# Decode attention with a gated MLP: output weights in two groups, and the first load in two parts

## The chip, the cores and the metric

The kernel runs on one core of one Trainium2 chip. The core has five engines that run beside each other: PE (matrix products), DVE (vector work), ACT (scalar functions and copies), POOL (small general work) and SP, which only issues transfers and waits. Sixteen DMA engines move data between the large memory outside (HBM) and the on-chip memory of 128 partitions (SBUF). A queue of transfers belongs to the engine that issues them; here SP's queue (q1 in the profile) carries nearly all bytes, ACT's (q10) a few small inputs.

The metric is device time in microseconds (us), as the median of several runs. Before the change it is 1311.9 us, with three runs between 1311.33 and 1311.93.

## The reference

One token for each of two sequences attends over a cache of 32768 keys; the result is projected, multiplied with a gate from a small MLP, and added to the input.

```python
xn = _layernorm(x)                                   # x: 2 x 1 x 512
q = (xn @ wq).reshape(B, Sq, 32, 128).transpose(...)  # 32 heads of 128
k = jnp.repeat(k_cache, 4, axis=1)                   # 8 key heads, 32768 x 128 each, twice
v = jnp.repeat(v_cache, 4, axis=1)
p = _softmax(einsum("bhqd,bhkd->bhqk", q, k) * 128 ** -0.5)
s = einsum("bhqk,bhkd->bhqd", p, v).reshape(B, Sq, 32 * 128) @ wo
h = xn @ w1 + b1
y = square(max(h, 0)) @ w2 + b2                      # 512 -> 1792 -> 512
return x + s * silu(y)
```

All is float32. The two caches are 537 MB of the 561 MB that are read.

## The kernel before

A *stage* is one sequence and one key head: 16 stages, `s` = 0 to 15. A stage has 16 MB of keys and 16 MB of values, which come in two transfers of 8 MB each (64 KB to a partition), numbered `m` = 0 to 31 for either. Keys go through a ring of three slots of 32 KB (`kslots`), values through one buffer of 64 KB (`vbuf`). For each quarter stage `n` (0 to 63), `scores` (L240) transposes the keys on DVE (L249) and multiplies on PE (L254); `softmax`, `probs` and `values` (L307) follow, with the product of probabilities and values at L315. After the last value product of a stage, L322 to L327 bring the four heads of that stage into `oT`. So far this runs for every stage.

The output projection needs `oT` spread in another layout. This is done for groups of `WG` = 8 heads: after every second key head (L328) one DVE product (L331, `om`), one PE product (L334) and one ACT copy (L335) fill `oW[:, i]` for one sequence. The small selection tables `selj` and `sele` (L175 to L178) are made once and have the group's shape. `oW` is used only at the end, by `project` (L394 to L398), which multiplies it with the output weights, group by group in the order 0, 1, 2, 3.

All large transfers are listed in order in `loads` (L137 to L142) and are issued by SP in that order; each has an event that it waits for, given by `give` when the last reader of its buffer has been written down. A transfer that waits holds all behind it. The first in the list is the query weights `wq` (`load_wq`, L87): 8 MB into all of `vbuf`, 64 KB to a partition, in one transfer. Then come the first key halves (L97), the MLP weights and the caches. Last are the value chunks 30 (into two key slots) and 31 (into `vbuf`), and the output weights: four groups of 2 MB (16 KB to a partition), groups 0 and 1 in the third key slot as soon as the last keys are used, groups 2 and 3 in the first key slot after the first half of value chunk 30 has been multiplied. Group 3 comes in four pieces, of 8, 4, 2 and 2 KB to a partition (`PIECES`, L34), so that little work is left after the last one:

```python
for i in range(NWG - 1):
    project(i, 0, WG)
for j0, j1 in PIECES:
    project(NWG - 1, j0, j1)
```

Then two DVE products (L406, L407) and two stores (L409) end the program. The order on each engine and all waits are made by a scheduler from the program's order; it gives each transfer of SP and ACT one of eight completion counters in turn, so that a transfer also waits until the one eight places before it has landed.

Of the kernel before, what the change touches and what calls it, by code (L numbers as in the profile page):

```python
# [14 lines left out]
P = 128  # L15
# [15 lines left out]
NT = 4  # L31
HALF = 64 * 128
NEG = -3.0e38
PIECES = ((0, 4), (4, 6), (6, 7), (7, 8))  # L34


@with_exitstack
def gqa_decode_kernel(ctx: ExitStack, tc: tile.TileContext, x, kc, vc, wq, wo, w1, b1, w2, b2, out):
    nc = tc.nc
    B, _, D = x.shape  # L40
    _, HKV, SK, DH = kc.shape
    HQ = wq.shape[1] // DH
    REP = HQ // HKV
    F = w1.shape[1]
    ND = D // P
    NS = B * HKV
    NCH = SK // CHUNK
    FG = F // NG
    FJ = FG // 32
    DE = D // NG  # L50
    WG = 8
    NWG = HQ // WG
    SCALE = 1.0 / math.sqrt(DH)
    assert 4 * REP == 16 and D == 512 and DH == P and REP * DH == 512 and NCH == 2 and F == P * FJ and WG == 2 * REP

    x2 = x.rearrange("b s d -> (b s) d")
    out2 = out.rearrange("b s d -> (b s) d")
# [7 lines left out]
    def misc(name):  # L65
        return pms.tile([P, 512], F32, tag="ms", name=name)
# [19 lines left out]

    def load_wq(_):  # L87
        t = vbuf.rearrange("p (d f) -> p d f", d=ND)
        nc.sync.dma_start(vbuf, wq.rearrange("(p d) f -> p (d f)", p=P))
        return t  # L90

    def key_slot(n):
# [26 lines left out]


    def load_wo(i):
        if i % 2 == 0:
            wide[i // 2] = kslots[:, 2 - i].rearrange("p (i j e) -> p i j e", i=2, j=WG)
        t = wide[i // 2][:, i % 2]
        src = wo[i * WG * P:(i + 1) * WG * P, :].rearrange("(p j) e -> p j e", p=P)
        if i < NWG - 1:
            nc.sync.dma_start(t, src)
        else:
            for j0, j1 in PIECES:
                nc.sync.dma_start(t[:, j0:j1, :], src[:, j0:j1, :])  # L130
        return t

    wide = {}
    NK, NV = NS * NT, NS * NCH
    kslots = const.tile([P, 3, HALF], F32, name="kslots")
    vbuf = const.tile([P, 2 * HALF], F32, name="vbuf")
    loads = [(None, load_wq, 0), (None, load_half, 0), (None, load_half, 1), (("q", 0), load_w1, 0),  # L137
             (("s", 0), load_half, 2), (None, load_half, 3), (("q", 0), load_w2, 0)]
    for m in range(2, NV):
        loads += [(("s", 2 * m - 2), load_k, m), (("v", m - 3) if m > 2 else ("w", 1), load_v, m - 2)]  # L140
    loads += [(("s", NK - 2), load_v, NV - 2), (("v", NV - 3), load_v, NV - 1)]
    loads += [(("s", NK - 1), load_wo, 0), (("s", NK - 1), load_wo, 1), (("v", NV - 2), load_wo, 2), (("v", NV - 2), load_wo, 3)]  # L142
    past = {None}
    done = [0]

# [6 lines left out]
    def take(f, a):  # L152
        return tiles.pop((f, a))

    def give(*event):
        past.add(event)
        issue()
# [15 lines left out]
    for t in qz:  # L173
        nc.gpsimd.memset(t, 0.0)
    selj = const.tile([P, WG], F32, name="selj")  # L175
    nc.vector.tensor_reduce(selj, ident.rearrange("p (e j) -> p j e", j=WG), axis=AX.X, op=ALU.add)
    sele = const.tile([P, P // WG], F32, name="sele")
# [27 lines left out]


    wqt = take(load_wq, 0)
    for d in range(ND):
        for f in range(2):
# [6 lines left out]
    for f in range(2):  # L216
        for h in range(REP):
# [6 lines left out]
            v = t_ps.rearrange("p (e g y) -> p g e y", e=4, g=NG)  # L224
# [82 lines left out]
    def values(n):  # L307
        s, k = divmod(n, NCH)
        vt = take(load_v, n)
        o = o_ps[s % 2]  # L310
        for c in range(2):
            for i in range(NO // 4):
                for g in range(NG):
                    lo = (c * NG + g) * NO + 4 * i
                    nc.tensor.matmul(o[32 * g:32 * g + 16, :], pT[s][:, k, c, g, 4 * i:4 * i + 4, :].rearrange("p o h -> p (o h)"),  # L315
                                     vt[:, lo:lo + 4, :].rearrange("p o d -> p (o d)"),
                                     start=(k + c + i == 0), stop=(k == NCH - 1 and c == 1 and i == NO // 4 - 1))
        give("v", n)
        if k == NCH - 1:
            hkv, b = divmod(s, B)  # L320
            o_sb = work.tile([P, 512], F32, tag="o_sb", bufs=1, name=f"o_sb{s}")
            nc.scalar.copy(o_sb, o)  # L322
            t_ps = misc(f"oT_ps{s}")
            r4 = rs.pop(s)
            for i in range(4):
                nc.tensor.matmul(t_ps[:, :REP], o_sb[:, i * DH:(i + 1) * DH], r4[:, i, :], start=(i == 0), stop=(i == 3))  # L326
            nc.vector.tensor_copy(oT[:, hkv * REP:(hkv + 1) * REP, b], t_ps[:, :REP])  # L327
            if hkv % 2 == 1:  # L328
                i = hkv // 2
                m = work.tile([P, WG, P // WG], F32, tag="om", bufs=1, name=f"om{s}")  # L330
                nc.vector.tensor_mul(m, oT[:, i * WG:(i + 1) * WG, b:b + 1].to_broadcast([P, WG, P // WG]),  # L331
                                     sele[:, None, :].to_broadcast([P, WG, P // WG]))
                t_ps = misc(f"oW_ps{s}")
                nc.tensor.matmul(t_ps[:, :WG], m.rearrange("p h e -> p (h e)"), selj, start=True, stop=True)  # L334
                nc.scalar.copy(oW[:, i, :, b], t_ps[:, :WG])  # L335
# [36 lines left out]
    for n in range(NK):  # L372
        s, i = divmod(n, NT)
        if i == 0:
            set_q(s)
        scores(n)
        if n == 1:
            mlp_up()
        if n == 3:
            mlp_down()  # L380
        if i == 3:
            softmax(s)
        if n >= 5 and n % 2 == 1:
            values((n - 5) // 2)
        if i == 3:
            probs(s)
    values(NV - 2)
    values(NV - 1)


    a_ps = sc[0]
    wot = [take(load_wo, i) for i in range(NWG)]

    def project(i, j0, j1):  # L394
        for j in range(j0, j1):
            for g in range(NG):
                nc.tensor.matmul(a_ps[32 * g:32 * g + 32, :DE], oW[:, i, j, :], wot[i][:, j, g * DE:(g + 1) * DE],  # L397
                                 start=(i == 0 and j == 0), stop=(i == NWG - 1 and j == WG - 1))  # L398
# [5 lines that stand above are left out]
# [29 lines left out]
```

## Time and profile before

| what | us |
|---|---|
| median of three runs | 1311.9 |
| the profiled execution's own time | 1312.29 |
| its span, first to last instruction | 1310.2 |
| PE busy | 912.5 |
| DVE busy | 669.9 |
| ACT busy | 130.3 |
| first transfer issued (L89) | 0.73 |
| query weights landed, first product with them (L212) | 22.79 |
| output weights: first of seven transfers issued | 1257.76 |
| last product of the projection done, DVE starts L406 | 1306.52 |

The profiled execution lies 0.4 us over the median; 2.1 us of it lie outside the span. In the lists of the profile a line gives the time of an operation's start in the span, its duration, the engine, the line of the program, and output and inputs; "x8" counts instructions. PE counts each product of float32 twice. SPq and ACTq are the two queues that issue transfers. In the table of windows the last three numbers of a row are PE's granted clock, the mean busy share of the sixteen DMA engines (packets are counted where they begin, so that a short window can show over 1.00) and the rate in GB/s.

### The profile page before, as it was taken

How to read it: one execution, taken by the hardware profiler on the slowest of the kernel's cores; microseconds unless marked ns; L12 is line 12 of the kernel's file. 1: busy time of each engine (PE TensorE's matmuls, PEld its weight loads, DVE VectorE, ACT ScalarE, POOL GpSimd, SP SyncE). 2: the span in 40 equal slices, each digit the busy share in tenths (PEclk: the TensorE clock that was granted, in tenths of full speed). 3: DMA queues.
4: the chain of work that ended last, by engine and by line, in shares of the span. 5: the costliest groups of instructions: out<-in, count | busy, mean ns of one | idle time of the engine just before them, and what ended most of it. 6: DMA issues, size and time to landing. Idle time of an engine off the chain costs nothing.

```text
span 1310.2 us, 11827 instructions
## 1 busy us (share of the span) xinstructions
PE 912.5 (70%) x5054; PEld 230.9 (18%) x5054; DVE 669.9 (51%) x778; ACT 130.3 (10%) x429; POOL 14.9 (1%) x76
## 2 busy tenths in 40 slices
PE   3777675758857677775758767576885767777575
PEld 1221121212202121120212112121220212111023
DVE  2866654446655445665445565444665544566410
ACT  0020010201002020110202001020110202001020
POOL 0000000000000000000000000000000000000000
PEclk9988877888878898887889878778987879888888
DMA  9999999999999999999999999999999999999997
GB/s 404 432 441 435 429 439 426 435 430 433 433 432 433 437 431 433 429 437 429 435 435 427 439 424 439 428 437 437 427 437 428 433 435 431 435 429 431 427 435 307
DMA packets 11042, 561.76 MB, mean 429 GB/s; under 512 B 1239, under 2 KB 1259, under 8 KB 1646
## 3 DMA queue, kind: packets, MB, share of 16 engines
q1 hardware_dynamic: 10952, 561.00, 99.2%
q8 instruction: 39, 0.64, 0.2%
q14 instruction: 13, 0.11, 0.0%
q10 hardware_dynamic: 38, 0.02, 0.0%
HBM read 561.01 MB, written 0.00 MB: 428 GB/s over the span
## 4 chain that ended last, share of the span: by engine, by line
DMA 72%; DVE 21%; issue 4%; PE 3%; ACT 0%; SPq 0%; DVEq 0%
DMA kslots<-in_A_k_cache 66%; DVE kt L249 20%; DMA kslots<-in_A_wo 2%; DMA kslots<-in_A_v_cache 2%; DMA vbuf<-in_A_wq 2%; PE sc L212 1%; PE sc L254 1%; PE o_ps L315 0%; PE y_ps L364 0%; PE h_ps L346 0%; ACT p L275 0%; DVE qr L219 0%; ACT pT L293 0%; PE pT_ps L289 0%; PE sc L397 0%
## 5 line engine op out<-in xcount | busy, mean ns | idle before, releaser
L254 PE MATMUL sc<-kt,qz 128*16 128x512 f32 x2048 | 574.4, 670 | 304.8 <-DVE kt L249 282.9
L249 DVE STREAM_TRANSPOSE kt<-kslots 128x1024 f32<-128x1024 f32 x512 | 583.8, 1206 | 300.5 <-DMA kslots<-in_A_k_cache 300.5
L315 PE MATMUL o_ps<-vbuf,pT 128*16 128x512 f32 x1984 | 232.3, 597 | 10.9 <-DMA vbuf<-in_A_v_cache 10.9
L254 PEld LDWEIGHTS sc<-kt,qz 128*16 128x16 f32 x2048 | 91.4, 98 | 772.8 <-DVE kt L249 619.0
L275 ACT ACTIVATE p<-sc,nm 128x512 f32<-128x512 f32 x64 | 45.7, 740 | 964.9 <-DVE nm L271 964.9
L315 PEld LDWEIGHTS o_ps<-vbuf,pT 128*16 128x16 f32 x1984 | 59.1, 97 | 160.8 <-issue 146.0
L258 DVE TENSOR_REDUCE rm<-sc 128x1 f32<-128x512 f32 x64 | 43.1, 673 | 66.3 <-PE sc L254 66.3
L293 ACT COPY pT<-pT_ps 64x128 f32<-64x128 f32 x256 | 66.4, 259 | 22.6 <-PE pT_ps L289 18.0
L289 PE MATMUL pT_ps<-ident,p 128*128 128x128 f32 x256 | 49.8, 342 | 18.1 <-ACT pT L293 13.8
L327 DVE COPY oT<-oT_ps 128x4 f32<-128x4 f32 x16 | 2.6, 162 | 97.9 <-PE oT_ps L326 97.9
L299 DVE RECIPROCAL r<-l_ps 128x4 f32<-128x4 f32 x16 | 2.9, 182 | 75.5 <-PE l_ps L297 75.5
L289 PEld LDWEIGHTS pT_ps<-ident,p 128*128 128x128 f32 x256 | 36.4, 177 | 28.0 <-ACT pT L293 23.5
L278 DVE TENSOR_REDUCE l<-l 128x1 f32<-128x4 f32 x16 | 2.5, 157 | 49.4 <-ACT p L275 49.4
L235 POOL COPY qz<-qT 32x16 f32<-32x16 f32 x64 | 12.7, 198 | 1078.2 <-PE sc L254 1043.0
L326 PE MATMUL oT_ps<-rs,o_sb 128*128 128x4 f32 x128 | 16.9, 255 | 11.5 <-ACT o_sb L322 11.4
L326 PEld LDWEIGHTS oT_ps<-rs,o_sb 128*128 128x128 f32 x128 | 15.5, 191 | 25.6 <-ACT o_sb L322 25.6
L322 ACT COPY o_sb<-o_ps 128x512 f32<-128x512 f32 x16 | 9.4, 585 | 76.9 <-PE o_ps L315 76.9
L264 PE MATMUL mx_ps<-ident,rm 128*128 128x128 f32 x16 | 5.2, 323 | 14.6 <-DVE rm L262 14.6
L203 PE MATMUL xnT_ps<-ident,xn 128*128 128x128 f32 x4 | 1.1, 431 | 20.1 <-DVE xn L199 20.1
L275 ACT ACTIVATION_READ_ACCUMULATOR p<-sc,nm 128x1 f32 x64 | 12.2, 191 | 0.0
L297 PE MATMUL l_ps<-lh,ones 128*128 128x4 f32 x32 | 8.4, 333 | 3.1 <-ACT pT L293 2.6
L212 PE MATMUL sc<-vbuf,first 128*32 128x512 f32 x64 | 9.4, 751 | 1.6 <-DMA vbuf<-in_A_wq 1.6
(69 smaller groups left out, 119.3 us busy)
## 6 DMA issues: line engine op xcount, KB each, us to landing
kslots<-in_A_k_cache SPq DMA_DIRECT2D x4, 4096.0 KB, 19.4
vbuf<-in_B_w SPq DMA_DIRECT2D x2, 3584.0 KB
kslots<-in_A_wo SPq DMA_DIRECT2D x3, 2048.0 KB
kslots<-in_A_wo SPq DMA_DIRECT2D x1, 1024.0 KB
kslots<-in_A_wo SPq DMA_DIRECT2D x1, 512.0 KB
kslots<-in_A_wo SPq DMA_DIRECT2D x2, 256.0 KB, 31.9
vbuf<-in_A_v_cache SPq DMA_DIRECT2D x31, 30.5
kslots<-in_A_k_cache SPq DMA_DIRECT2D x30
```

The costliest lines, as they stand in the source:

```text
L212: nc.tensor.matmul(sc[f][32 * g:32 * g + 32, :], xnT[:, d, 0:32], wqt[:, d, cc * 512:(cc + 1) * 512], start=(d == 0), stop=(d == ND - 1))
L235: nc.gpsimd.tensor_copy(qz[s % 2][32 * a:32 * a + 32, :, a * REP:(a + 1) * REP], qT[32 * a:32 * a + 32, b, hkv].rearrange("p h e -> p e h"))
L249: nc.vector.transpose(r.rearrange("p e o w -> p o e w"), kt[:, g * NO:(g + 1) * NO, e0 * 32:(e0 + 2) * 32].rearrange("p o (e w) -> p o e w ...
L254: nc.tensor.matmul(sc[t][32 * g:32 * g + 4 * REP, :], qz[s % 2][:, e0 + e, :], kts[g][:, e].rearrange("p o w -> p (o w)"), start=(e0 + e = ...
L258: nc.vector.tensor_reduce(rm[s][:, t:t + 1], sc[t], axis=AX.X, op=ALU.max)
L275: nc.scalar.activation(p[:, :, t % 2, :, t // 2], sc[t].rearrange("p (o w) -> p o w", w=32), AF.Exp, bias=nm, scale=SCALE, accum_out=l4[:, ...
L289: nc.tensor.transpose(t_ps[:, j * P:(j + 1) * P], p[:, 4 * i + j].rearrange("p c w u -> p (c w u)"), ident)
L293: nc.scalar.copy(sb[64 * a:64 * a + 64, :, c, :, 4 * i:4 * i + 4, :].rearrange("p k g o h -> p o g k h"), v[:, :, :, :4 * REP].rearrange(" ...
L297: nc.tensor.matmul(t_ps[:, :REP], ones, lh, start=True, stop=True)
L315: nc.tensor.matmul(o[32 * g:32 * g + 16, :], pT[s][:, k, c, g, 4 * i:4 * i + 4, :].rearrange("p o h -> p (o h)"), vt[:, lo:lo + 4, :].rear ...
L322: nc.scalar.copy(o_sb, o)
L326: nc.tensor.matmul(t_ps[:, :REP], o_sb[:, i * DH:(i + 1) * DH], r4[:, i, :], start=(i == 0), stop=(i == 3))
```

## The change

There are two edits. The output weights are taken in two groups of 16 heads in place of four of 8. Group 0 is one transfer of 4 MB (32 KB to a partition) into the third key slot; group 1 comes in five pieces, of 16, 8, 4, 2 and 2 KB to a partition, into the first key slot. The spreading (L331 to L335) is done for 16 heads at a time, and `selj`, `sele` and `oW` change their shapes with it. Since a partition now holds 16 rows of `wo` that follow each other in HBM, and not 8, the pairing of rows and partitions differs, in the weights and in `oW` alike.

And the query weights, the first load of all, come in two transfers: partitions 0 to 15, then partitions 16 to 127.

```diff
-PIECES = ((0, 4), (4, 6), (6, 7), (7, 8))
+PIECES = ((0, 8), (8, 12), (12, 14), (14, 15), (15, 16))
...
-    WG = 8
+    WG = 16
     NWG = HQ // WG
...
     def load_wq(_):
         t = vbuf.rearrange("p (d f) -> p d f", d=ND)
-        nc.sync.dma_start(vbuf, wq.rearrange("(p d) f -> p (d f)", p=P))
+        src = wq.rearrange("(p d) f -> p (d f)", p=P)
+        for p0, p1 in ((0, 16), (16, P)):
+            nc.sync.dma_start(vbuf[p0:p1], src[p0:p1])
         return t
...
     def load_wo(i):
-        if i % 2 == 0:
-            wide[i // 2] = kslots[:, 2 - i].rearrange("p (i j e) -> p i j e", i=2, j=WG)
-        t = wide[i // 2][:, i % 2]
+        t = kslots[:, 2 - 2 * i].rearrange("p (j e) -> p j e", j=WG)
         src = wo[i * WG * P:(i + 1) * WG * P, :].rearrange("(p j) e -> p j e", p=P)
         if i < NWG - 1:
             nc.sync.dma_start(t, src)
...
-    loads += [(("s", NK - 1), load_wo, 0), (("s", NK - 1), load_wo, 1), (("v", NV - 2), load_wo, 2), (("v", NV - 2), load_wo, 3)]
+    loads += [(("s", NK - 1), load_wo, 0), (("v", NV - 2), load_wo, 1)]
...
-            if hkv % 2 == 1:
-                i = hkv // 2
+            if hkv % 4 == 3:
+                i = hkv // 4
```

More of the change, by code (lines that the diff above doesn't have):

```diff
@@ L50, in gqa_decode_kernel @@
     DE = D // NG
-    WG = 8
+    WG = 16
     NWG = HQ // WG
     SCALE = 1.0 / math.sqrt(DH)
-    assert 4 * REP == 16 and D == 512 and DH == P and REP * DH == 512 and NCH == 2 and F == P * FJ and WG == 2 * REP
+    assert 4 * REP == 16 and D == 512 and DH == P and REP * DH == 512 and NCH == 2 and F == P * FJ and WG == 4 * REP
     x2 = x.rearrange("b s d -> (b s) d")
@@ L131, in load_wo @@
         return t
-    wide = {}
     NK, NV = NS * NT, NS * NCH
```

## The prediction

> **What bounds the kernel now.** I read the page first. DVE, the second busiest engine, works half of the span, PE 70%, and the row of the DMA engines shows 9, over 90%, in every slice but the last:
>
> ```profile
> span 1310.2 us, 11827 instructions
> PE 912.5 (70%) x5054; PEld 230.9 (18%) x5054; DVE 669.9 (51%) x778; ACT 130.3 (10%) x429; POOL 14.9 (1%) x76
> ...
> DMA  9999999999999999999999999999999999999997
> ...
> HBM read 561.01 MB, written 0.00 MB: 428 GB/s over the span
> ```
>
> Then the table of windows, cut where the transfers begin, where the first load has landed, and where they thin out at the end:
>
> ```profile
> 0.00:1.70 1.70, 0.00 (x0) 0.00 (x0) 0.69 (x2) 0.00 (x0) 1.09 (x10) 1.00 0.00 1
> 1.70:22.40 20.70, 1.10 (x4) 0.73 (x4) 6.88 (x17) 1.49 (x2) 1.17 (x3) 1.00 1.03 431
> 22.40:1299.00 1276.60, 904.83 (x4862) 225.25 (x4866) 661.71 (x758) 128.81 (x427) 12.68 (x64) 0.85 1.00 432
> 1299.00:1305.60 6.60, 5.76 (x189) 4.66 (x179) 0.00 (x0) 0.00 (x0) 0.00 (x0) 1.00 0.50 202
> 1305.60:1310.20 4.60, 0.83 (x16) 0.29 (x10) 0.58 (x2) 0.00 (x0) 0.00 (x0) 1.00 0.00 1
> ```
>
> This decides the case. From 1.7 to 1299 us all sixteen DMA engines are busy (share 1.00) at 432 GB/s. There is no gap into which a delay of the transfers could go, and no computing to be saved. What the change can move is the 1.7 us ahead of the first byte, the rate of the first load, and the last 11 us. A microsecond lost by the slowest DMA engine at the start comes out at the end.
>
> The list in order of time, then SP's waits, for the start:
>
> ```profile
> 0.73 0.39 SPq L89 DMA_DIRECT2D vbuf<-in_A_wq  x1
> 2.29 20.70 SPq L97 DMA_DIRECT2D kslots<-in_A_k_cache  x2
> 15.31 0.69 DVE L191 TENSOR_REDUCE st<-first 128x1 f32<-128x512 f32 x1 [11.71 <-DMA first<-in_A_x]
> 21.26 0.69 DVE L204 COPY first<-xnT_ps 128x512 f32<-128x512 f32 x1 [1.29 <-PE xnT_ps L203]
> 22.79 9.37 PE L212 MATMUL sc<-vbuf,first 128*32 128x512 f32 x64 [1.56 <-DMA vbuf<-in_A_wq]
> ```
> ```profile
> SPq L97 <- DMA vbuf<-in_A_wq: 20.0, 1, 20.0
> ...
> SPq L97 <- DMA b1t<-in_B_b: 1.2, 1, 1.2
> ```
>
> The input x is ready for PE at 21.95, the query weights at 22.79: the first load leads by 0.8. And for the end, where the last value products and the output weights meet:
>
> ```profile
> 1298.37 0.17 ACT L335 COPY oW<-oW_ps 128x8 f32<-128x8 f32 x1 [2.25 <-PE oW_ps L334]
> 1301.06 1.69 PEld L397 LDWEIGHTS sc<-kslots,oW 128*32 128x32 f32 x64 [0.46 <-DMA kslots<-in_A_wo]
> ...
> 1306.52 0.29 DVE L406 TENSOR_TENSOR a_sb<-gate,sc 128x128 f32<-128x128 f32 x1 [8.76 <-PE sc L397]
> ```
>
> PE waits for group 2 until 1301.06, then for pieces of group 3.
>
> **The output weights.** The same 8.4 MB come in six transfers, not seven, into the same slots after the same releases, and the last piece is again 2 KB to a partition, so that the same PE work is left behind it. One issue less on SP (0.44 by the chain, 1272.45) is covered: SP then stands ahead of transfers that are queued. I take 0; the ends are that one issue, -0.4, and the wait of PE named next, +0.4. The spreading is done 4 times, not 8: four DVE products of 0.29, four ACT copies of 0.17 and eight PE products of 0.26 go. Three of the four pairs of places lie deep in the stream, where DVE is idle half of the time: 0. The last one stays. It is ready at 1298.37 + 0.17 = 1298.54; now the first piece of group 1 needs it where group 2 did not, but that piece lands at 1301.06, 2.5 later. All of group 0 now waits for 4 MB; its second half is what group 1 was, and PE had finished both by 1300.6 (1301.06 less the 0.46 it waited). If that cover is gone, the pieces behind take up the first tenths: 0 to +0.4. The tables `selj` and `sele` (0.37 and 0.28 on DVE at 18.8) lie in a chain that ends 0.8 ahead of the query weights: 0.
>
> **One transfer more at the start.** SP issues twice, 0.39 each, into a queue that has 20 us to work off: 0. The completion counters shift by one: now the first key half waits for the first transfer on the chip (1.2) and the second for the query weights (20.0). Afterwards they wait for a part of 16 rows and for the other part or a small input. If the first key half fell behind the whole of the query weights, a gap as at the start would open, 1.7 - 0.73 = 1.0, and 0.3 for the landing: 0 to +1.3. The part of 16 rows lands far ahead of that: 0. PE waits for two counters ahead of L212: under 0.1.
>
> **The rate of 16 rows.** This is the term that counts. All large loads of this trace fill 128 rows, and the rate is the same whatever the piece. At 432 GB/s sixteen engines take 65,536 x 16 / 432 = 2.43 us for one row of 64 KB each; 8 rows each are the 19.4 us of the first load. With 16 rows each engine has one row, then seven. If the rate belongs to the engines, this costs nothing, and shorter lists could bring the first byte sooner, at most by the 1.0 between issue and first byte. If it belongs to the rows written, 16 rows get a share of it. The trace has one row near this: from 1299 on half of the engines are done (share 0.50) and the rate is 202, half of 432. The others do not speed up; what limits is not HBM but something that each engine has to itself, or the eight rows it fills. The row fits both readings.
>
> Ends: -1.0 (earlier start, rate of the engines), and +19.4: each partition takes only 1/128 of the rate, so that 16 rows last the full 19.4 and the 112 rows 19.4 more. Between them I take a limit by groups of eight rows, as the tail row has it, and sixteen neighbouring rows spread over four of the sixteen groups: between two groups (no spread, 8 x 2.43 = 19.4) and sixteen (2.43). Four engines then share each, and the part takes 4 x 2.43 = 9.7. In this time the twelve other groups receive nothing and have all of their 19.4 ahead: +9.7. The 112 rows go to engines in sevens, which no longer are the groups of eight; engines meet at a group between never and three times, 2.43 each, 0 to +7.3 for the slowest. I take one: +2.4. Together +12.1, own range +7.3 (only the engines' lost time, 9.7 - 2.4, counts) to +19.4.
>
> [...]
>
> **What follows the first load.** The chain to PE (L191 to L204, 6.6 us) starts when x lands, about two thirds of the way through the first load (15.3 of 22.6); with a load of 34 us that is 23 + 6.6 = 29.6: covered. The second key half, the MLP weights and all behind move with the load's landing, and DMA stays the bound.
>
> Sum against the profiled execution's 1312.3: 12.1 + 0 + 0 gives 1324.4. The median is 0.4 lower, so 1324.0.
>
> **The rivals.**
>
> 1. *The rate belongs to the engines.* For it: each engine has one row, the share is 1.00 at every size of piece. Against it: no row shows fewer partitions at that rate. Then the sum is between -1.0 and +1.3: 1310.9 to 1313.2, most likely 1311.7. The part that it is about would do nothing.
> 2. *The engines meet at every row.* If the 112 rows are dealt so that neighbouring rows are always in flight together, all eight rows take 9.7: 8 x 9.7 - 19.4 = +58, 1370; with a part of that 1331 and more. Against it: engines drift apart (they end between 1299 and 1305.5).
> 3. *Faster: the end evens out.* From 1299 to 1305.6 half of the rate is lost: 6.6 x (1 - 202 / 432) = 3.5 us. If the new division of rows put the engine that ends last ahead, and the 16 rows cost nothing, the time would be 1308.4. It decides from 2.6 us on. Against it: every engine still has eight rows; bytes per engine do not change.
>
> **How the numbers follow.** What the trace leaves open reaches from -1.0 to +19.4, and 0.2% is 2.6 us, about what a measurement of this kernel can tell from no change; (19.4 - 2.6) / 20.4 = 82% of it lies above. I take some off, since the trace is as well explained by engines. Limit by groups of rows, 1319.2 to 1331.3: 0.64. Rival 1: 0.20. Rival 2: 0.08. Rival 3: 0.05. A small delay between 1313 and 1319, by a gap or a milder sharing: 0.03, of which 0.01 is within 0.2%. So faster 0.05, same 0.21, slower 0.74. The range is 1310.5 to 1331.5: it takes in rival 1 and leaves out rivals 2 and 3, 0.13.
>
> **What the changed profile would show.** The first product of L212 starts near 35 and not 22.8; the window from 1.7 to 12 moves about 110 GB/s at a full share; from there to 1299 + 12 the rate is 432 again; the wait of PE at the first piece, the 1306.52 and the stores keep their distances to the last landing, all 12 later. L331, L334, L335 appear 4, 8 and 4 times. I am wrong if L212 starts within 1 us of 22.8, or if a delay of L212 does not come out at the end, which would need a gap in the stream that I do not see.

## The result, and the profile after

The changed kernel takes 1334.81 us (median of four runs, 1332.97 to 1335.59) against 1311.91 beside it: 22.9 us more, by the record 1.0171 times the time before, with a 95% interval of 1.0158 to 1.0183. (The ratios in this text are the record's and can differ a little from those of the medians.) The sign and the place are as forecast; the size is nearly twice the forecast 12.1, and lies outside the range.

The table of windows of the changed kernel, cut again where the transfers begin, about where the first part and the second part of the first load end, and where the transfers thin out and stop (engine by engine, then PE's granted clock, the share of the DMA engines, GB/s):

```profile
1.70:11.30 9.60, 0.00 (x0) 0.00 (x0) 1.74 (x4) 1.28 (x1) 1.17 (x3) 1.00 1.46 213
11.30:43.00 31.70, 1.10 (x4) 0.73 (x4) 5.13 (x13) 0.20 (x1) 0.00 (x0) 1.00 0.88 221
43.00:1319.00 1276.00, 896.41 (x4814) 218.99 (x4818) 660.47 (x754) 128.16 (x423) 12.69 (x64) 0.86 1.00 432
1319.00:1325.40 6.40, 4.33 (x140) 4.06 (x136) 0.00 (x0) 0.00 (x0) 0.00 (x0) 0.91 0.51 204
1325.40:1333.10 7.70, 3.96 (x104) 3.69 (x96) 0.58 (x2) 0.00 (x0) 0.00 (x0) 0.86 0.00 1
```

Up to 43 us the DMA engines are busy, but move half as much as before (213 and 221 GB/s against 431); a busy share does not say that bytes move. The 213 is not the 110 that I forecast for the first part, because packets are counted where they begin: by the packets of the trace 15 rows of the second part began before 11.3. The first part's own 1.05 MB in 9.6 us are 109 GB/s. From 43 on the rows are those of before: 432 GB/s for 1276 us, then six microseconds at half of it. The shift of 20.0 at the thinning (1299 to 1319) and of 19.8 at the stop (1305.6 to 1325.4) came in with the first load, whose delay of 21.9 at the first product is still mostly there at the end.

The list in order of time, the lines that answer to those of the start and of the end:

```profile
0.73 1.90 SPq L91 DMA_DIRECT2D vbuf<-in_A_wq  x2
12.61 0.69 DVE L190 TENSOR_REDUCE st<-first 128x1 f32<-128x512 f32 x1 [9.00 <-DMA first<-in_A_x]
13.11 0.83 SPq L99 DMA_DIRECT2D kslots<-in_A_k_cache  x2
44.70 8.49 PE L211 MATMUL sc<-vbuf,first 128*32 128x512 f32 x64 [26.20 <-issue]
...
1318.21 3.70 PE L396 MATMUL sc<-kslots,oW 128*32 128x128 f32 x128
1323.99 5.37 PE L396 MATMUL sc<-kslots,oW 128*32 128x128 f32 x128 [2.08 <-issue]
1329.42 0.29 DVE L405 TENSOR_TENSOR a_sb<-gate,sc 128x128 f32<-128x128 f32 x1 [11.65 <-PE sc L396]
```

The first product with the query weights starts at 44.70, 21.9 later than at 22.79. Both key halves are issued together at 13.11, soon after the first part is down: the shifted counters made nothing late. And at the end there is something that was not there before. PE stands from 1321.91 to 1323.99, then needs 5.37 us for its 128 products (before: 2.87 for the last 64 and 1.95 for the 64 ahead of them), and is done 4.0 after the transfers stop; before the change it was 1306.5 against 1305.6. In this trace, then, 19.8 of the 22.9 is transfers and 3.1 is PE's end. How much belongs to which edit is another question, and comes next.

### The profile page after: what moved, and what is told of

It is laid out like the page before. It is cut to its first block, busy times and chain, and to the rows that moved or that the text cites. A ratio compares the mean times of both kernels' runs of the same rounds, so it can differ in the third digit from the quotient of the medians.

```text
span 1333.1 us, 11797 instructions
## 1 busy us (share of the span) xinstructions
PE 905.8 (68%) x5046; PEld 227.5 (17%) x5046; DVE 668.6 (50%) x774; ACT 129.6 (10%) x425; POOL 14.9 (1%) x76
## 4 chain that ended last, share of the span: by engine, by line
DMA 67%; DVE 21%; issue 6%; PE 4%; ACT 1%; ACTq 0%; DVEq 0%
DMA kslots<-in_A_k_cache 64%; DVE kt L248 20%; DMA vbuf<-in_A_v_cache 2%; PE o_ps L314 1%; DMA first<-in_A_x 1%; PE sc L396 1%; PE sc L253 1%; PE sc L211 1%; PE y_ps L363 0%; PE h_ps L345 0%; ACT p L274 0%; DVE qr L218 0%; PE pT_ps L288 0%; ACT pT L292 0%; DVE rm L257 0%
## 5 line engine op out<-in xcount | busy, mean ns | idle before, releaser
L288 PE MATMUL pT_ps<-ident,p 128*128 128x128 f32 x256 | 46.1, 323 | 19.9 <-ACT pT L292 15.5
L211 PE MATMUL sc<-vbuf,first 128*32 128x512 f32 x64 | 8.5, 690 | 26.2 <-issue 26.2
L325 PE MATMUL oT_ps<-rs,o_sb 128*128 128x4 f32 x128 | 16.9, 255 | 12.4 <-ACT o_sb L321 12.4
L218 DVE COPY qr<-sc 128x512 f32<-128x512 f32 x8 | 5.2, 679 | 33.5 <-PE sc L211 33.2
L274 ACT ACTIVATION_READ_ACCUMULATOR p<-sc,nm 128x1 f32 x64 | 12.1, 190 | 0.0
```

Source lines behind the costliest of these rows:

```text
L211: nc.tensor.matmul(sc[f][32 * g:32 * g + 32, :], xnT[:, d, 0:32], wqt[:, d, cc * 512:(cc + 1) * 512], start=(d == 0), stop=(d == ND - 1))
L274: nc.scalar.activation(p[:, :, t % 2, :, t // 2], sc[t].rearrange("p (o w) -> p o w", w=32), AF.Exp, bias=nm, scale=SCALE, accum_out=l4[:, ...
L288: nc.tensor.transpose(t_ps[:, j * P:(j + 1) * P], p[:, 4 * i + j].rearrange("p c w u -> p (c w u)"), ident)
```

## The experiments

Each was run beside the kernel before on the same chip; the ratios are to that.

### The two edits alone

The first kernel has the change's two transfers of the first load and the old output weights, the second the reverse.

```diff
 # e1_wq_only, against the kernel before
-        nc.sync.dma_start(vbuf, wq.rearrange("(p d) f -> p (d f)", p=P))
+        src = wq.rearrange("(p d) f -> p (d f)", p=P)
+        for p0, p1 in ((0, 16), (16, P)):
+            nc.sync.dma_start(vbuf[p0:p1], src[p0:p1])
 # e1_wo_only, against the changed kernel
-        src = wq.rearrange("(p d) f -> p (d f)", p=P)
-        for p0, p1 in ((0, 16), (16, P)):
-            nc.sync.dma_start(vbuf[p0:p1], src[p0:p1])
+        nc.sync.dma_start(vbuf, wq.rearrange("(p d) f -> p (d f)", p=P))
```

> The first load in parts of 16 and 112 partitions, the output weights as before. Theory (rows written): everything that the change cost at the start is here, the first product of the query stage 21.9 us later than before; the end of the transfers 19.8 later, as in the changed kernel, and the work behind the last landing as short as before, so 1331 to 1332. Rival (the two edits work on each other through the completion counters): less than half of the 22.9.

> The output weights in two groups, the first load as before. In the changed kernel PE stood still for 2.08 us between the two groups (1321.91 to 1323.99) and the transfers had ended 4.0 before the last product, against 1.0 before the change. Theory: this belongs to the new grouping, so 1313.5 to 1315.5. Rival (it belongs to the delayed start, through the drifted engines): 1311.5 to 1312.3. My forecast's step said 0 with ends of -0.4 and +0.4.

The first load in two parts alone: 1333.17 us, ratio 1.0161 (1.0147 to 1.0174), 20.9 more than the 1312.24 of before, and 1.2 above my range; the first product starts at 44.86. The end of this kernel, on PE:

```profile
1327.61 0.42 PE L399 MATMUL sc<-kslots,oW 128*32 128x128 f32 x8 [0.21 <-DMA kslots<-in_A_wo]
```

PE waits for the last piece and is done at 1328.0, 21.5 later than before, and by the packets the transfers stop at 1327.1, 21.6 later, not 19.8 as I expected. So the delay of the first load comes out at the end almost whole, and the 19.8 and 3.1 of the changed kernel are not the shares of the two edits.

The output weights alone: 1313.35, ratio 1.0010 (1.0001 to 1.0019), 1.1 more, with runs between 1312.0 and 1315.9. The two together are 22.0 of the 22.9. The first edit is the cost; the second has a small one of its own, less than I expected from the pause in the changed kernel's trace and more than the rival allowed.

### The same bytes, by columns

A second transfer at the start could cost by being a second transfer. This one moves 1 MB and 7 MB too, each over all partitions.

```diff
-        nc.sync.dma_start(vbuf, wq.rearrange("(p d) f -> p (d f)", p=P))
+        src = wq.rearrange("(p d) f -> p (d f)", p=P)
+        for c0, c1 in ((0, 2048), (2048, 16384)):
+            nc.sync.dma_start(vbuf[:, c0:c1], src[:, c0:c1])
```

> The first load in two transfers that move the same 1 MB and 7 MB as the changed kernel, but both of 128 partitions: 8 KB of each partition, then 56 KB of each. Output weights as before. Theory (rows written): both run at the full rate, 1311.4 to 1312.6, the first product within 0.6 of 22.8. Rival (a second transfer at the start costs, through its issue, its counter, or the small inputs behind it): 1320 and more, first product after 30.

1311.76, ratio 0.9997 (0.9988 to 1.0006): nothing. The list of this kernel shows that the first part is even used, without a gain:

```profile
16.36 1.94 PE L214 MATMUL sc<-vbuf,first 128*32 128x512 f32 x8 [0.78 <-DVE first L206]
22.60 7.68 PE L214 MATMUL sc<-vbuf,first 128*32 128x512 f32 x56 [4.30 <-DMA vbuf<-in_A_wq]
```

PE begins at 16.36 in place of 22.79, earlier than I expected, and waits again. So neither the number of transfers nor the shifted counters cost anything, and an earlier start of PE is worth nothing either, since the transfers set the time.

### A ladder of loads

Ten loads of the query weights' buffer go ahead of the kernel before, in one execution. Each overlaps the one before it and waits for its landing (the first, issued at 0.73, landed 21.90 later; the second was issued at 22.65); the real load comes last. The time from issue to issue is then a load's price, some 2.5 us of it fixed, by an estimate from 21.9 for 128 rows, whose bytes take 19.4 at the 432 GB/s of the long stretch.

```diff
+        src = wq.rearrange("(p d) f -> p (d f)", p=P)
+        nc.sync.dma_start(vbuf, src)                    # L90
+        nc.sync.dma_start(vbuf[16:P], src[16:P])
+        nc.sync.dma_start(vbuf[0:P:8], src[0:16])
+        nc.sync.dma_start(vbuf[0:16], src[0:16])        # L93
+        nc.sync.dma_start(vbuf[0:32:2], src[0:16])
+        nc.sync.dma_start(vbuf[0:106:7], src[0:16])     # L95
+        nc.sync.dma_start(vbuf[0:16], src[0:P:8])       # L96
+        nc.sync.dma_start(vbuf[0:64], src[0:64])        # L97
+        nc.sync.dma_start(vbuf[0:P:2], src[0:64])       # L98
+        nc.sync.dma_start(vbuf[0:112], src[0:112])      # L99
         nc.sync.dma_start(vbuf, wq.rearrange(...))      # L100
```

> Ten transfers into the query weights' buffer, one after the other, ahead of the kernel before: 64 KB to a partition each, and then the query weights as before over all of it. Time from one issue to the next, of which some 3 us are fixed. Theory (what counts is which partitions are written): 128 rows 22; rows into partitions 16 to 127: 34; 16 rows into every eighth partition: 8; into partitions 0 to 15: 13; into every second of 32: 8; into every seventh of 106: 6 to 8; 16 rows from every eighth place of the source into partitions 0 to 15: 13 again; 64 rows into partitions 0 to 63: 22; into every second of 128: 13 to 22; 112 rows into partitions 0 to 111: 34. Rival (source: 16 or 112 neighbouring 64 KB pieces of the outer memory are slow): the four loads from source rows 0 to 15 all 13, the one from every eighth source row 6, both 64-row loads alike. Rival (only the number of rows counts): all loads of 16 rows 13, both of 64 alike.

The key halves slipped in between the first five, which I had overlooked (each is 9.7 us of bytes); from L95 on the steps are clean. SP's list of this run:

```profile
120.05 0.52 SPq L95 DMA_DIRECT2D vbuf<-in_A_wq  x1
127.12 0.34 SPq L96 DMA_DIRECT2D vbuf<-in_A_wq  x1
138.69 0.51 SPq L97 DMA_DIRECT2D vbuf<-in_A_wq  x1
161.51 0.51 SPq L98 DMA_DIRECT2D vbuf<-in_A_wq  x1
173.95 0.33 SPq L99 DMA_DIRECT2D vbuf<-in_A_wq  x1
206.54 0.35 SPq L100 DMA_DIRECT2D vbuf<-in_A_wq  x1
```

Subtract neighbouring starts. Sixteen rows into every seventh partition: 7.1. Sixteen rows *from* every eighth place of the source into partitions 0 to 15: 11.6; the source does not decide, against the first rival. Sixty-four rows into partitions 0 to 63: 22.8, as long as 128 rows; into every second partition: 12.4, half of it; the same source rows and the same number, against the second rival. For loads of 16 and of 64 rows, which partitions are written decides. 112 rows: 32.6.

### A second ladder, and real kernels with 64 rows

The second ladder, again one execution, starts with four full loads, so that the key halves are out of the way of all steps but the first. It asks how a load's time goes with the number and the place of the partitions written, and whether the 32.6 of 112 rows comes again.

```diff
+        src = wq.rearrange("(p d) f -> p (d f)", p=P)
+        for _ in range(4):
+            nc.sync.dma_start(vbuf, src)
+        nc.sync.dma_start(vbuf[0:16], src[0:16])        # L92
+        nc.sync.dma_start(vbuf[0:P:8], src[0:16])       # L93
+        nc.sync.dma_start(vbuf[16:P], src[16:P])        # L94
+        nc.sync.dma_start(vbuf[0:96], src[0:96])        # L95
+        nc.sync.dma_start(vbuf[0:96:2], src[0:48])      # L96
+        nc.sync.dma_start(vbuf[0:32], src[0:32])        # L97
+        nc.sync.dma_start(vbuf[0:P:4], src[0:32])       # L98
+        nc.sync.dma_start(vbuf[0:32:2], src[0:16])      # L99
+        nc.sync.dma_start(vbuf[0:112], src[0:112])      # L100
```

> A second ladder, now with four full loads first, so that no key load lies between the steps measured. From issue to issue, 2 to 3 us of it fixed. [...]

```profile
129.93 0.62 SPq L93 DMA_DIRECT2D vbuf<-in_A_wq  x1
137.35 0.32 SPq L94 DMA_DIRECT2D vbuf<-in_A_wq  x1
170.59 0.31 SPq L95 DMA_DIRECT2D vbuf<-in_A_wq  x1
202.76 0.54 SPq L96 DMA_DIRECT2D vbuf<-in_A_wq  x1
220.11 0.32 SPq L97 DMA_DIRECT2D vbuf<-in_A_wq  x1
232.54 0.51 SPq L98 DMA_DIRECT2D vbuf<-in_A_wq  x1
240.52 0.52 SPq L99 DMA_DIRECT2D vbuf<-in_A_wq  x1
248.03 0.32 SPq L100 DMA_DIRECT2D vbuf<-in_A_wq  x1
280.83 0.35 SPq L101 DMA_DIRECT2D vbuf<-in_A_wq  x1
```

| rows, into partitions | at 432 GB/s | measured |
|---|---|---|
| 16, every eighth (L93) | 4.9 | 7.4 |
| 16, every second of 32 (L99) | 4.9 | 7.5 |
| 32, every fourth (L98) | 7.4 | 8.0 |
| 32, 0 to 31 (L97) | 7.4 | 12.4 |
| 48, every second of 96 (L96) | 9.8 | 17.3 |
| 96, 0 to 95 (L95) | 17.1 | 32.2 |
| 112, 16 to 127 (L94) | 19.5 | 33.2 |
| 112, 0 to 111 (L100) | 19.5 | 32.8 |

The second column is an estimate: 2.43 for every sixteen rows, the bytes at 432 GB/s, and the 2.5 fixed. Only the 32 rows into every fourth partition come near it, as the 64 rows into every second did in the first ladder (12.4, by the same estimate 12.2). The place counts again: 32 rows take 8.0 or 12.4. Less the 2.5 fixed, 32 neighbours, 48, 96 and 112 rows take 5.0, 4.9, 4.9 and 4.3 to 4.4 us for every sixteen rows, nearly twice 2.43. The table of windows says the same in rates, for L94 and for L98:

```profile
138.30:170.00 31.70, 0.00 (x0) 0.00 (x0) 0.00 (x0) 0.00 (x0) 0.00 (x0) 1.00 0.95 232
...
233.80:240.20 6.40, 0.00 (x0) 0.00 (x0) 0.00 (x0) 0.00 (x0) 0.00 (x0) 1.00 0.88 328
```

112 rows run at 232 GB/s with the DMA engines busy; the 32 scattered rows at 328, in a window that also takes in their beginning and end. Why these loads are slow is not shown: which engine takes which row is not in the trace. Nor was the source varied for these counts: it was a run of neighbouring rows each time.

Then the two places of 64 rows in the kernel itself, in each of two transfers (against the kernel before; `src` as above):

```diff
 # e2_evenodd
+        for k in range(2):
+            nc.sync.dma_start(vbuf[k:P:2], src[k:P:2])
 # e2_halves
+        for p0, p1 in ((0, 64), (64, P)):
+            nc.sync.dma_start(vbuf[p0:p1], src[p0:p1])
```

> The first load in two transfers of 64 rows, the even partitions and then the odd ones; output weights as before. Theory (which partitions are written): 64 rows into every second partition took 12.4 us in the ladder, half of a full load's 21.9 with the fixed part, so two behind each other keep the full rate: 1311.4 to 1313, first product within 1 us of 22.8. Rival (fewer than 128 rows are slow): as the next one, 1331 to 1335.

> The first load in two transfers of 64 rows, partitions 0 to 63 and then 64 to 127; output weights as before. Theory (which partitions are written): 64 rows into partitions 0 to 63 moved for 20.7 us in the ladder, as long as 128 rows, so the two last 41.5 and all comes 20 to 22 later: 1331 to 1335, first product at 43 to 45. Rival (the slow thing is the uneven division, 112 rows in sevens, and not the partitions): 1312 to 1314.

Even and odd partitions: 1312.54, ratio 1.0001 (0.9992 to 1.0010), first product at 23.25. Lower and upper half, in two runs: 1333.2, ratio 1.0161 (1.0142 to 1.0179), first product at 44.26. The windows of the first load, of the even and odd rows and of the halves:

```profile
1.70:22.40 20.70, 1.10 (x4) 0.73 (x4) 6.88 (x17) 1.49 (x2) 1.18 (x3) 1.00 1.00 419
```
```profile
1.70:22.40 20.70, 0.00 (x0) 0.00 (x0) 1.74 (x4) 1.28 (x1) 1.17 (x3) 1.00 1.04 216
22.40:43.00 20.60, 1.10 (x4) 0.73 (x4) 5.14 (x13) 0.20 (x1) 0.00 (x0) 1.00 0.99 210
```

Two transfers of the same sizes from the same tensor, 419 against 216 GB/s. This settles that the partitions written, and not the number or the size of the transfers, set the rate of the first load. For the 112 rows of the change it leaves a gap: that such a load takes 33 us is measured three times (32.6, 33.2, 32.8), and no run shows why.

### The end

In the run with the new output weights alone PE began to project only after the last spreading, and was slow at first (the last line is a row of the table of windows):

```profile
1296.79 1.06 PE L323 MATMUL oT_ps<-rs,o_sb 128*128 128x4 f32 x8 [0.77 <-ACT o_sb L319]
1298.52 0.56 PE L331 MATMUL oW_ps<-selj,om 128*128 128x16 f32 x2 [0.67 <-DVE om L328]
1299.01 5.12 PE L394 MATMUL sc<-kslots,oW 128*32 128x128 f32 x128
...
1299.00:1301.00 2.00, 2.00 (x41) 1.85 (x44) 0.00 (x0) 0.19 (x1) 0.00 (x0) 0.50 0.61 256
```

The clock was granted at 0.50 from 1299 to 1301. The changed kernel did its first 128 products in 3.70 us, at 1.00, so that some 1.4 of the 5.12 go with the half clock, an estimate from these two rows. Before the change 40 of the products lay in PE's pauses between the last steps of the attention:

```profile
1295.23 0.82 PE L397 MATMUL sc<-kslots,oW 128*32 128x128 f32 x18
1296.17 1.05 PE L326 MATMUL oT_ps<-rs,o_sb 128*128 128x4 f32 x8
1297.16 0.86 PE L397 MATMUL sc<-kslots,oW 128*32 128x128 f32 x22
```

There group 0 had landed, by the packets of the trace, at 1287.7; with one transfer its 4 MB land whole at 1295.5. Here the two pauses last from 1296.0 to 1296.8 and from 1297.85 to 1298.5, so that the weights were there, just ahead of the first and over 2 us ahead of the second. PE projects in neither: in the order that the scheduler gave this program the products stand behind the spreading (1299.01, after 1298.52). The next kernel keeps the grouping and lets group 0 come in two transfers.

```diff
 # against the run with the output weights alone
         if i < NWG - 1:
-            nc.sync.dma_start(t, src)
+            for j0, j1 in ((0, 8), (8, 16)):
+                nc.sync.dma_start(t[:, j0:j1, :], src[:, j0:j1, :])
```

> The output weights in two groups as in the change, but group 0 in two transfers of 2 MB; the first load as before. In the run with the two groups alone, PE began the projection at 1299.01, after all of the last spreading, and had 128 products behind each other; before, 40 of them lay in the pauses from 1295.2 on, as group 0 had landed at 1287.7 and not at 1295.5. Theory (the late landing of 4 MB in one transfer keeps PE from starting): 1311.6 to 1312.6. Rival (the grouping itself, by the order of the work on PE): 1313 to 1314, as with the two groups alone.

1311.92, ratio 0.9996 (0.9987 to 1.0005), with runs of 1311.6 to 1312.5, and the products are back in the pauses:

```profile
1295.04 0.82 PE L395 MATMUL sc<-kslots,oW 128*32 128x128 f32 x18
1295.98 1.05 PE L324 MATMUL oT_ps<-rs,o_sb 128*128 128x4 f32 x8
1296.96 0.85 PE L395 MATMUL sc<-kslots,oW 128*32 128x128 f32 x22
...
1298.08 2.61 PE L395 MATMUL sc<-kslots,oW 128*32 128x128 f32 x88
...
1306.27 0.43 PE L395 MATMUL sc<-kslots,oW 128*32 128x128 f32 x8 [0.21 <-DMA kslots<-in_A_wo]
```

PE again waits for the last piece, and not the end for PE. The two intervals (1.0001 to 1.0019 and 0.9987 to 1.0005) overlap, so that the effect is small beside the noise, but the lists differ where the theory says. Its reason holds only in part: the one transfer of 4 MB goes with the late start, but through the order of the products on PE, since the weights were there in the pauses. Why the scheduler ordered them so was not looked into. In this run the 88 products go at full speed (2.61 us, as before the change); the early start and the full clock come back together, and no run parts them.

### Both edits, mended

The first load by columns and group 0 in two transfers, in one kernel (the two diffs above together).

> Both edits of the change in the forms that cost nothing alone: the first load split by columns (8 KB, then 56 KB of all 128 partitions) and group 0 of the output weights in two transfers of 2 MB. Theory (the cost of the change lay wholly in the partitions of the first load and in the late landing of group 0): 1311.4 to 1312.6, no difference from before. Rival (some of the 22.9 comes from both edits together, as by the shifted completion counters): 1314 and more. A gain of over 0.2% would need the transfers to end earlier, which nothing so far shows.

1311.35, ratio 0.9995 (0.9986 to 1.0004). Nothing is left of the 22.9. Its runs lie low (1311.2 to 1311.8, against 1311.4 to 1312.6 for the kernel before beside it), but the interval takes in 1: no version here is shown to beat the kernel before.

## Why the prediction was wrong

**What held.** The transfers are the bound (432 GB/s at a busy share of 1.00 from 43 to 1319), and a delay of the first load comes out at the end: with the first edit alone 21.6 at the stop of the transfers, in the changed kernel 21.9 at the first product and 19.8 at the stop. Where those 2.1 went was not looked into. The second edit's parts counted as 0 (six issues, four spreadings less) show nothing of their own; L330, L333 and L334 appear 4, 8 and 4 times. The chain of x was covered, with more room than I gave it: x landed at 12.6, earlier than before. The choice of rows written over engines, on which the sign hung, was right, in part by luck: for it I had the tail's row, which fitted both, and a guess. That sixteen neighbouring rows lie in four of sixteen groups, from which the 9.7 of the sum was worked out, is shown by no run. What the runs show is the time: partitions 0 to 15 took 9.6 us for 1.05 MB in the changed kernel, 109 GB/s, and 11.6 - 2.5 = 9.1 us in the ladder, 115 GB/s, where 16 rows into every eighth partition took 7.4 - 2.5 = 4.9. And 64 neighbouring partitions were hardly faster than 32: 216 GB/s in the halves, against 212 for the 32 rows of the ladder (2.1 MB in 12.4 - 2.5 us).

**The step that failed** is "engines meet at a group between never and three times, 2.43 each, 0 to +7.3 for the slowest. I take one: +2.4." The first part did as worked out: the 16 rows were down at 11.3, 9.6 after the first byte, where I had 9.7. The 112 rows took from there, by the packets, to 43.6: 32.3 us in place of 7 x 2.43 = 17.0. That is +15.3 where I had +2.4. Taken by sixteens in the order of their starts, the 112 rows took between 3.2 and 5.6 us each in the mean, and the shortest single one 2.8. The upper end of three meetings was drawn from nothing in the trace, and so was the upper end of the whole, +19.4, that took 1/128 of the rate for each partition as the worst that could be. Rival 2 had the time ("with a part of that 1331 and more") and put it down to engines that meet at every row; in full it was priced at 9.7 us a row, +58, where the 32.3 us for seven rows are 4.6 a row. It had 0.08. That the engines meet is not shown, so that the reason for the 15.3 stays open; its size is what the ladders show again, 32.6 to 33.2 us for 112 rows. With the first part's own loss of 9.6 - 2.4 = 7.2 the sum is 22.5, near the 21.9 that L211 shows.

**The output weights** were a smaller miss. I wrote that PE "had finished both by 1300.6" (1300.87 by its products, 1298.26 + 2.61), and took the pieces' landing as the only thing that could follow. The cover rested on the 40 products in the pauses between the last steps of the attention, and on the full clock behind them; with one transfer of 4 MB both were gone. The term is +1.1 (0.1 to 2.5 by its interval), against my ends of -0.4 and +0.4. In the changed kernel PE's end cost 3.1. Its pause of 2.08 ahead of the second group, from 1321.91, has no releaser in the profile, and by the packets the first piece of that group was down at 1320.4. A transfer of instructions (queue q8) begins shortly before the pause, at 1321.4, and ends in it, and PE's clock is granted at about half from 1324 to 1327 after it. Neither was taken away in a run, so this part stays open.

**The chances.** Slower, which came, had 0.74; the range was too narrow on the side where the mechanism was unknown.

## What to carry to other kernels

In these runs a load's time went with the partitions that it wrote, and not with its bytes alone: 64 rows took 22.8 us into partitions 0 to 63 and 12.4 into every second one, and 96 and 112 rows took 32.2 and 32.8 where all 128 took 21.9. So before splitting a transfer by partitions, measure the split, and where one is wanted, try it by columns, or by even and odd partitions, which cost nothing here (ratios 0.9997 and 1.0001). A transfer that runs beside nothing need not be at full speed: read GB/s beside the busy share, which was 0.88 and more at half the rate here (213 and 221 GB/s, against 432). And before merging two transfers, look for what is done with the first while the second is still on its way, and where the scheduler then puts it.

## What the runs showed that I had not expected

48 rows into every second of 96 partitions took 17.3 us, where 64 rows into every second of 128 took 12.4; and 112 rows took half as long again as 128 (32.8 against 21.9). And 64 rows into every second partition ran at the full rate, 419 GB/s in the kernel, so that full speed does not need all 128 partitions in one transfer.
